# Smaller PE tiles in the first group, and weight loads on one queue, in a fused mLSTM and SwiGLU kernel

## The chip, the cores and the metric

The kernel runs on one core of a Trainium2 chip. Its time is device microseconds; three runs of the kernel before gave 514.97, 515.15 and 516.0, a median of 515.15. The engines are named as in the profile: PE (TensorE, matmuls), PEld (its weight loads), DVE (VectorE), ACT (ScalarE), POOL (GpSimd) and SP (SyncE, which here only issues transfers). ACT issues some transfers too. Each engine works through its own instructions in the order in which the program writes them.

## The reference

Two blocks follow each other. The first is an mLSTM cell over batch 4, 8 heads, 768 steps, head size 40; the second a SwiGLU feed-forward on its output, 3072 tokens of 320 features, hidden size 1536. All is float32.

```python
for t in range(S):
    kt, vt, qt = (k[:, :, t], v[:, :, t], q[:, :, t])
    m_new = np.maximum(f_gate[:, :, t] + m, i_gate[:, :, t])
    f_stab = np.exp(f_gate[:, :, t] + m - m_new)
    i_stab = np.exp(i_gate[:, :, t] - m_new)
    m = m_new
    C = f_stab[..., None, None] * C + i_stab[..., None, None] * np.einsum('bhd,bhe->bhde', vt, kt)
    n = f_stab[:, :, None] * n + i_stab[:, :, None] * kt
    h_tilde = np.einsum('bhde,bhe->bhd', C, qt)
    denom = np.maximum(np.abs(np.einsum('bhd,bhd->bh', n, qt)[:, :, None]), 1.0)
    y[:, :, t] = 1.0 / (1.0 + np.exp(-o_gate[:, :, t])) * h_tilde / denom
...
g = x @ w_gate
silu = g * (1.0 / (1.0 + np.exp(-g)))
return (silu * (x @ w_val)) @ w_out
```

The feed-forward weights reach the kernel as 64-bit floats in pairs of 32-bit words; the kernel makes float32 of them itself.

## The kernel before

**Groups.** The 768 steps are cut into six groups of 128 tokens (of each of the four sequences, so 512 tokens). For each group the kernel does the cell in chunk form (scores of k and q, decay weights, a product with v, and a state carried from chunk to chunk), turns the result x to features on partitions (xT), multiplies it with the gate and value weights, and the hidden values with the output weights. The cell of the next group is worked into the feed-forward of the one before. Groups 1 to 5 do their feed-forward products with seven half-size products in place of eight (`gated`, `project_seven`); group 0 does them plainly (`hidden` for each of 12 blocks m of 128 hidden features, then `project_all`).

**First group.** It has nothing to hide behind. Heads are handled in two halves P=0 and P=1 (sequences u=0, 1 and u=2, 3), 16 heads each. The steps named below are: `first_mask`, `first_inputs`, `first_maxima`, `first_exp` (the 128x128 decay weights W0, kept in h_sb[0:8]), `first_turn` (k and q to kT and qT, eight 128x128 transposes for each P and tensor, copied out of PSUM by two engines), `first_scores` (kT by qT, then DVE multiplies into W0), `first_own(u)` (W0 by v, 8 matmuls of 128x128 stationary and 41 moving columns in float32), `first_x(u)` (denominator and division on DVE), `first_gate(P)` (times the output gate), `first_seam(P)` (x to xT, ten 128x128 transposes), `first_state(P)` (k by weighted v, 128x64 tiles), `first_kept` (its copy to the state ring). `burn(n)` runs n bfloat16 matmuls whose result nobody reads. Later groups use forms of the same steps on 64-row tiles: `turn_one` and `seam`.

**PSUM.** Two rings of four banks: "cell" and "gen". `hidden(m)` takes two "gen" banks, so block m waits for the banks of block m-2, which are free when ACT (SiLU, line 688) and DVE (product, line 689) have read them. Scores and `add` share the "cell" ring.

**Weights.** They come in ten pieces (`PIECES`): pieces 0 and 1 are gate and value blocks 0 and 1, pieces 2 to 6 two blocks each (1280 KB), pieces 7 to 9 output weights. `piece_load` issues three transfers for a gate and value piece: the gate half to partitions 0 to 63 on SP, and the value half to partitions 64 to 127 in two transfers, on ACT for pieces 0 to 4 and on SP for the others. A piece lands in a raw buffer (a ring of two, `conv`) or in a "home" that is not used yet: h_sb[1:6] for piece 2, h_sb[8:13] for piece 3, wo_sb for piece 4. A block is then converted: `scale` on ACT (two instructions, lines 211 and 213), `join` on DVE (lines 220 and 221), `rounded` on POOL or DVE (line 228).

**Group 1 inside group 0's projections.** After each `hidden(0, m)` the list `slots[m]` is issued. Its order is the order on SP's queue as well. `late_sums` and `late_maxima` make M_sb, the running maxima of the later groups; these are written to a tensor in HBM (M_dram, line 933) and read back spread over partitions by `weights_load` (line 479) into w_sb. Slot 7 subtracts and masks w_sb (lines 483 and 488), slot 8 takes the exponential (line 492) and weighs the values, slot 9 does scores and multiplies them into w_sb (line 359), slot 10 runs `add` (line 378), slot 11 `attend`. `ahead[m]` names the blocks converted between the matmuls of m and its SiLU; block 8 is converted in m=5.

Of the kernel before, what the change touches and what calls it, by code (L numbers as in the profile page):

```python
# [12 lines left out]
U32 = mybir.dt.uint32  # L13
# [5 lines left out]
L = 128  # L19
# [5 lines left out]
def kernel(  # L25
# [50 lines left out]
    def bank(name, tag="cell"):  # L76
        return psum.tile([128, 512], F32, name=name, tag=tag)
# [77 lines left out]


    raws = {}
    PIECES = [("gv", 0, 1), ("gv", 1, 1)] + [("gv", m, 2) for m in range(2, NFC, 2)] + [("o", m, 4) for m in range(0, NFC, 4)]

    def piece_load(p, home=None):  # L160
        kind, m, n = PIECES[p]
        if kind == "gv":
            a, d = NKC, n * 128
            gate_w, val_w = (w[:, m * 128:(m + n) * 128].rearrange("(c p) f -> p c f", p=HP) for w in (moe_w_gate, moe_w_val))
            src = [(slice(0, HP), slice(0, NKC), gate_w), (slice(HP, 128), slice(0, NKC - 1), val_w[:, 1:]),
                   (slice(HP, 128), slice(NKC - 1, NKC), val_w[:, 0:1])]
            queues = (nc.sync,) + 2 * (nc.scalar if p < 5 else nc.sync,)
        else:
            a, d = n, DM
            src = [(slice(0, 128), slice(0, n), moe_w_out[m * 128:(m + n) * 128].rearrange("(a p) d -> p a d", p=128))]  # L170
            queues = (nc.sync,)
        if src[0][2].dtype == F32:
            for r, cs, w in src:
                if kind == "o":
                    nc.sync.dma_start(out=wo_sb[r, m:m + n, :], in_=w)
                else:
                    for x in range(n):
                        nc.sync.dma_start(out=wgv_sb[r, m + x, cs], in_=w[:, :, ts(x, 128)])
            return
        if home is None:  # L180
            raw = conv.tile([128, 4 * NKC * 128], U32, name="raw")
        else:
            raw = home.rearrange("p a t -> p (a t)").bitcast(U32)
        raw = raw[:, 0:2 * a * d]
        for (r, cs, w), queue in zip(src, queues):
            queue.dma_start(out=raw[r].rearrange("p (a d) -> p a d", a=a)[:, cs], in_=w.bitcast(U32))
# [122 lines left out]
    M_dram = tc.dram_tile([BH, S - L], F32, name="M_dram")  # L309


    def turn_one(P, src, dst, engs):
        tp = [bank("tp_kq").rearrange("p (a t) -> p a t", t=SUB) for _ in range(2)]
# [146 lines left out]
    def xT(n):  # L460
        return xT_sb
# [74 lines left out]
    def first_turn(P, src, dst, engs):  # L536
        for b in range(2):
            tp = bank("tp_kq").rearrange("p (a t) -> p a t", t=L)
            for a in range(UA // 2):
                h = P * UH + b * H + 2 * a  # L540
                nc.tensor.transpose(tp[:, a, :], src[:, h:h + 2, :].rearrange("p h d -> p (h d)"), ident)  # L541
            a = P * UA + b * UA // 2
            copy(engs[b], dst[:, a:a + UA // 2, :], tp)

    def first_scores(P):
# [13 lines left out]
    def first_own(u):  # L559
        first_y[u] = bank("first_y", "gen")[:, 0:H * D1].rearrange("p (h d) -> p h d", d=D1)  # L560
        for h in range(H):
            nc.tensor.matmul(first_y[u][:, h, :], lhsT=W0[:, u * H + h, :], rhs=v_sb[:, u * H + h, :], start=True, stop=True)  # L562

    def first_x(u):
        y = first_y.pop(u)
# [7 lines left out]
    def first_gate(P):  # L573
        for u in (2 * P, 2 * P + 1):
            x = x_sb[:, u, 0:DM].rearrange("p (h d) -> p h d", d=D)
            nc.vector.tensor_tensor(x, x, o_sb[:, u * H:(u + 1) * H], op=ALU.mult)
# [10 lines left out]
    def first_kept(P, ps, eng):  # L587
        copy(eng, state(2)[:, P * UA:(P + 1) * UA], ps)

    def first_seam(P, engs):  # L590
        for c, eng in zip(range(0, NKC, 2), engs):
            cs = range(c, min(c + 2, NKC))
            tp = bank("tp_x")[:, 0:len(cs) * 2 * L].rearrange("p (c u s) -> p c u s", u=2, s=L)
            for w in cs:
                for b in range(2):
                    nc.tensor.transpose(tp[:, w - c, b, :], x_sb[:, 2 * P + b, ds(w * HP, 2 * HP)], ident)
            copy(eng, xT(0)[:, c:c + len(cs), 2 * P * L:(2 * P + 2) * L].rearrange("p c (u s) -> p c u s", u=2), tp)
# [48 lines left out]
    piece_load(5)  # L646


    pair = early.tile([BH, PP], F32)
# [279 lines left out]
    def load_all(dst, a, n):  # L929
        for P in range(2):  # L930
# [7 lines left out]
    ahead[0] = []  # L938
    ahead.update({4: [6], 5: [7, 8], 6: [9], 7: [10], 8: [11], 9: [], 10: [], 11: []})
    slots = {  # L940
        0: [run(convert, 2, V), run(late_maxima), run(load_all, k_sb, k, 1),
            run(nc.sync.dma_start, out=M_dram, in_=flat(M_sb)), run(load_all, q_sb, q, 1)],
        1: [run(piece_load, 6), run(late_decay)],
        2: [run(nc.scalar.activation, step1, step1, AF.Exp), run(decay_rows), run(weights_load, 1), run(load_all, v_sb, v, 1)],
        3: [run(late_turns)],
        4: [run(decay)],
        5: [run(turn, 0, (A, A), (A, V))],
        6: [run(turn, 1, (A, A), (A, V)), run(piece_load, 7)],
        7: [run(weights_sub, 1, 0), run(weights_mask, 0), run(weights_sub, 1, 1), run(weights_mask, 1), run(nc.gpsimd.memset, q_sb, 0.0)],
        8: [run(weights_exp, 0), run(weights_exp, 1), run(weigh_values, G, 0), run(weigh_values, G, 1),  # L950
# [124 lines left out]
```

## Time and profile before

| | us |
|---|---|
| median of three runs (514.97 to 516.0) | 515.15 |
| the profiled execution | 516.62 |
| its span, first to last instruction | 514.8 |
| start of the first projection (line 683) | 31.62 |
| end of group 0's plain feed-forward, start of the first L831 | 126.2 |
| granted TensorE clock, share of full | 0.998 |

A line of a timeline gives the start, the length, the engine, the line of the program, the operation, what is written and read, the shapes and how many; in brackets, the idle time of the engine before it and who ended it. A group's length runs from its first start to its last end, so it can hold waits. SPq and ACTq are the queues that issue transfers: their length is the issue, not the transfer. The view of a line's instructions gives the time from issue to landing.

Waits of the first 95 us that bear on the parts that are changed:

```profile
ACT o_sb L495 <- DMA raw<-in_moe_w_val_dram: 4.7, 1, 4.7
...
DVE w_sb L483 <- DMA w_sb<-M_dram: 1.4, 1, 1.4
```

The columns are: who waited for whom, the sum in us, how often, the longest.

### The profile page before, as it was taken

The numbers are of one execution on the slowest core, as the hardware profiler recorded it, in microseconds if no ns is written. First come the engines' busy times: TensorE is split into PE (matmuls) and PEld (weight loads), VectorE is DVE, ScalarE is ACT, GpSimd is POOL, SyncE is SP. The second block draws the span as 40 slices with busy tenths as digits, with TensorE's granted clock in tenths as the row PEclk, the third lists the DMA queues.
The fourth block names the chain that finished last, engine by engine and source line by source line (L and its number), as shares of the span: only waits on it lengthen the run. The fifth ranks groups of instructions, "written<-read, shape, count | busy, mean of one in ns | idle before, by whom it ended". The sixth has DMA issues, their size and how long they took to land.

```text
span 514.8 us, 14725 instructions
## 1 busy us (share of the span) xinstructions
PE 506.3 (98%) x6309; PEld 430.3 (84%) x6309; DVE 345.3 (67%) x547; ACT 179.7 (35%) x269; POOL 279.2 (54%) x283
## 2 busy tenths in 40 slices
PE   8999999999999999999999999999999999999997
PEld 4964445667888889898899898999898899988896
DVE  5779666899858879857669656659666754233421
ACT  3377555434222244322335322345231330123210
POOL 1303327566399789457657457657347750166710
PEclk9999999999999999999999999999999999999999
DMA  9999999698100866700886600896700210100001
GB/s 126 176 241 221 171 215 216 148 180 94 52 3 12 153 101 76 105 3 6 132 127 76 107 3 3 122 138 77 108 4 1 34 21 20 33 1 1 0 14 39
DMA packets 205497, 43.28 MB, mean 84 GB/s; under 512 B 193432, under 2 KB 200600, under 8 KB 205432
## 3 DMA queue, kind: packets, MB, share of 16 engines
q1 hardware_dynamic: 203444, 39.49, 47.7%
q10 hardware_dynamic: 1988, 2.85, 2.4%
q8 instruction: 50, 0.82, 0.7%
q14 instruction: 15, 0.12, 0.1%
HBM read 35.68 MB, written 4.01 MB: 77 GB/s over the span
## 4 chain that ended last, share of the span: by engine, by line
PE 77%; DVE 11%; POOL 4%; issue 3%; DMA 2%; ACT 2%; SPq 1%; DVEq 0%; ACTq 0%; POOLq 0%
PE gv_x L831 23%; PE o_ps L754 20%; PE gv_y L831 18%; PE gv_ps L683 5%; DMA w_sb<-M_dram 2%; PE inter L401 2%; PE intra L406 2%; PE sp L352 2%; PE first_y L562 1%; POOL w_sb L488 1%; PE burn L501 1%; DVE vw_sb L419 1%; POOL tmp L872 1%; PE tp_kq L541 1%; PE sp L551 1%
## 5 line engine op out<-in xcount | busy, mean ns | idle before, releaser
L831 PE MATMUL gv_x<-xT,wgv_sb 64*128 64x256 f32 x720 | 93.7, 382 | 0.7 <-ACT tmp L881 0.4
L831 PEld LDWEIGHTS gv_x<-xT,wgv_sb 64*128 64x128 f32 x720 | 69.0, 187 | 9.0 <-issue 1.1
L754 PE MATMUL o_ps<-wo_sb,h_sb 128*128 128x160 f32 x480 | 67.4, 300 | 0.0
L754 PEld LDWEIGHTS o_ps<-wo_sb,h_sb 128*128 128x128 f32 x480 | 65.6, 190 | 1.7 <-issue 1.7
L683 PE MATMUL gv_ps<-xT,wgv_sb 64*128 64x512 f32 x240 | 53.5, 595 | 0.3 <-DVE wgv_sb L228 0.3
L488 POOL TENSOR_SCALAR_AFFINE_SELECT w_sb<-w_sb 64x1024 f32<-64x1024 f32 x20 | 31.1, 1555 | 25.3 <-DVE w_sb L483 16.8
L683 PEld LDWEIGHTS gv_ps<-xT,wgv_sb 64*128 64x128 f32 x240 | 23.5, 187 | 25.0 <-issue 23.5
L831 PE MATMUL gv_y<-q_sb,wgv_sb 64*128 64x256 f32 x360 | 44.1, 377 | 0.3 <-DVE x_sb L871 0.3
L831 PE MATMUL gv_y<-xT,wgv_sb 64*128 64x256 f32 x360 | 44.0, 376 | 0.0
L879 ACT ACTIVATE h_sb<-gv_x 128x256 f32<-128x256 f32 x30 | 11.5, 384 | 86.3 <-PE gv_x L831 86.2
L831 PEld LDWEIGHTS gv_y<-q_sb,wgv_sb 64*128 64x128 f32 x360 | 35.3, 187 | 4.2 <-DVE x_sb L871 0.7
L831 PEld LDWEIGHTS gv_y<-xT,wgv_sb 64*128 64x128 f32 x360 | 35.5, 187 | 3.4
L754 PE MATMUL o_ps<-wT,S 128*128 128x160 f32 x240 | 33.5, 300 | 0.1
L754 PEld LDWEIGHTS o_ps<-wT,S 128*128 128x128 f32 x240 | 32.8, 190 | 0.4 <-DVE tmp L768 0.4
L871 DVE TENSOR_TENSOR tmp<-tmp,gv_y 128x1024 f32<-128x1024 f32 x15 | 18.3, 1220 | 20.2 <-PE gv_y L831 18.3
L872 POOL TENSOR_TENSOR tmp<-tmp 128x512 f32<-128x512 f32 x15 | 20.0, 1335 | 21.1 <-DVE tmp L871 21.1
L831 PE MATMUL gv_x<-q_sb,sw 64*128 64x256 f32 x240 | 31.0, 376 | 0.0
L852 POOL TENSOR_TENSOR h_sb<-tmp 128x512 f32<-128x512 f32 x13 | 16.7, 1287 | 25.5 <-ACT tmp L851 25.5
L871 DVE TENSOR_TENSOR x_sb<-x_sb,gv_y 128x1024 f32<-128x1024 f32 x15 | 18.3, 1218 | 17.0 <-PE gv_y L831 16.1
L861 ACT COPY tmp<-gv_x 128x1024 f32<-128x1024 f32 x15 | 15.2, 1012 | 40.5 <-PE gv_x L831 40.5
L721 POOL TENSOR_TENSOR S<-h_sb 128x256 f32<-128x256 f32 x30 | 22.8, 759 | 9.2 <-DVE h_sb L852 7.3
L723 POOL TENSOR_TENSOR S<-S,h_sb 128x256 f32<-128x256 f32 x30 | 27.3, 911 | 0.0
(216 smaller groups left out, 1004.2 us busy)
## 6 DMA issues: line engine op xcount, KB each, us to landing
w_sb<-M_dram SPq DMA_DIRECT2D x10, 512.0 KB, 7.3
k_sb<-in_k_dram SPq DMA_DIRECT2D x12, 320.0 KB, 6.5
v_sb<-in_v_dram SPq DMA_DIRECT2D x12, 320.0 KB, 5.8
o_sb<-in_o_gate_dram SPq DMA_DIRECT2D x12, 320.0 KB, 6.3
raw<-in_moe_w_out_dram SPq DMA_DIRECT2D x3, 1280.0 KB, 7.6
x_sq<-k_sb SPq DMA_DIRECT2D x64, 40.0 KB, 2.0
q_sb<-in_q_dram SPq DMA_DIRECT2D x32, 64.0 KB, 2.5
out_dram<-tmp SPq DMA_DIRECT2D x24, 80.0 KB, 2.8
```

What stands on the lines that cost most here:

```text
L352: nc.tensor.matmul(sp[two][half(i), a, :], lhsT=kT[feats(two), P * UA + a, half(i)], rhs=qT[feats(two), P * UA + a, half(i)], start=True, ...
L488: nc.gpsimd.affine_select(w, w, compare_op=ALU.is_ge, fill=NEG, base=0, pattern=[[0, UH], [1, SUB]], channel_multiplier=-1)
L683: nc.tensor.matmul(ps[i], lhsT=wgv_sb[half(i), m, kc, :], rhs=x[half(i), kc, :], start=(kc == 0), stop=(kc == NKC - 1))
L721: eng.tensor_tensor(S1[:, k], lo[:, second_half], hi[:, second_half], op=ALU.add)
L723: eng.tensor_tensor(S2[:, k], S1[:, k], lo[:, first_half], op=ALU.subtract)
L754: nc.tensor.matmul(node[x][:, i], lhsT=lhs(k)[:, ts(i, L)], rhs=rhs(k), start=start and k == 0 and i == 0, stop=stop and k == KH - 1, skip ...
L831: nc.tensor.matmul(ps[:, i, cols], lhsT=lhs(c)[half(i)], rhs=rhs(c)[half(i)], start=start and c == 0, stop=stop and c == n - 1, skip_group ...
L852: (nc.vector if k == KH - 1 else nc.gpsimd).tensor_tensor(h_sb[:, 2 * k + 1], uw[:, 0], uw[:, 1], op=ALU.mult)
L861: nc.scalar.copy(uw, x)
L871: nc.vector.tensor_tensor(uw, uw, y, op=ALU.add)
L872: nc.gpsimd.tensor_tensor(uw[:, :, second_half], uw[:, :, second_half], uw[:, :, first_half], op=ALU.add)
L879: nc.scalar.activation(h[:, first_half], x[:, 0, first_half], AF.Silu)
```

## The change

Eight edits, in the diff below:

- `first_turn` is left for P=0 only; P=1 is turned by `turn_one`, sixteen 64-row transposes each for k and q.
- The 128x128 transposes of `first_seam` are gone; `seam` (twenty 64x64 tiles) does x for both P.
- `first_own` does each head in two halves of 64 columns, 16 matmuls for each u in place of 8.
- `first_gate` takes an engine: POOL for P=0, DVE for P=1.
- Burns are put in more places, 25 matmuls in all where there were 13; most go to the "gen" ring.
- All weight transfers are issued on SP's queue.
- Piece 1 shares piece 0's raw buffer, pieces 2 and 6 land in a free stretch of wo_sb (`spare_wo`), piece 4 in the raw ring.
- `late_sums` moves to the end of the first group, `late_maxima` from slot 0 to slot 1, `late_decay` from slot 1 to slot 2; piece 5 is issued in slot 0 behind the loads of k and q; M_dram is written in slot 1 behind piece 6, and its load stays in slot 2.

```diff
-            queues = (nc.sync,) + 2 * (nc.scalar if p < 5 else nc.sync,)
+            queues = (nc.sync,) + (nc.sync, nc.sync)
...
         if home is None:
-            raw = conv.tile([128, 4 * NKC * 128], U32, name="raw")
+            if p != 1:
+                raw = conv.tile([128, 4 * NKC * 128], U32, name="raw")
+                ring[p] = raw
+            else:
+                raw = ring[0][:, 2 * NKC * 128:]
...
+    spare_wo = wo_sb.rearrange("p m d -> p (m d)")[:, H * L:H * L + 4 * NKC * 128].rearrange("p (a t) -> p a t", a=1)
...
         for h in range(H):
-            nc.tensor.matmul(first_y[u][:, h, :], lhsT=W0[:, u * H + h, :], rhs=v_sb[:, u * H + h, :], start=True, stop=True)
+            for i in range(2):
+                nc.tensor.matmul(first_y[u][half(i), h, :], lhsT=W0[:, u * H + h, half(i)], rhs=v_sb[:, u * H + h, :],
+                                 start=True, stop=True)
...
-    first_turn(0, k_sb, kT, (V, V))
-    first_turn(0, q_sb, qT, (A, V))
+    first_turn(k_sb, kT, (V, V))
+    first_turn(q_sb, qT, (A, V))
     first_exp(1)
     first_values(0)
     first_scores(0)
-    first_own(0)
-    late_sums()
-    first_turn(1, k_sb, kT, (A, A))
-    first_x(0)
-    first_turn(1, q_sb, qT, (A, V))
+    burn(2, "gen")
+    turn_one(1, k_sb, kT, (A, A))
     load(o_sb, o_gate, 0, 1)
     piece_load(0)
+    burn(1, "gen")
+    first_own(0)
     first_own(1)
+    turn_one(1, q_sb, qT, (A, V))
     first_values(1)
+    first_x(0)
+    first_x(1)
+    burn(4, "gen")
     first_scores(1)
-    first_x(1)
     sig(0)
     piece_load(1)
-    burn(3)
+    piece_load(2, spare_wo)
+    burn(3, "gen")
     first_own(2)
-    piece_load(2, h_sb[:, 1:1 + NKC])
+    burn(1, "gen")
+    first_own(3)
+    first_gate(0, G)
     sig(1)
-    burn(2)
-    first_own(3)
-    first_gate(0)
+    seam(0, 0, (A, A, A, A))
     first_x(2)
     first_x(3)
-    first_gate(1)
-    first_seam(0, (A, A, V))
+    first_gate(1, V)
     scale(0)
-    ps1 = first_state(1, "gen")
-    burn(1, "gen")
+    states = [first_state(P, "gen") for P in range(2)]
+    burn(2, "gen")
     piece_load(3, h_sb[:, NH - NKC:])
     join(0)
-    first_seam(1, (A, A, V))
     rounded(0, V)
-    first_kept(0, first_state(0), A)
-    first_kept(1, ps1, V)
+    seam(0, 1, (A, V, A, V))
+    burn(5, "gen")
+    first_kept(0, states[0], A)
+    first_kept(1, states[1], V)
+    piece_load(4)
     convert(1, V)
+    late_sums()
     nc.scalar.activation(warm, warm, AF.Silu)
-    piece_load(4, wo_sb)
-    piece_load(5)
...
-        0: [run(convert, 2, V), run(late_maxima), run(load_all, k_sb, k, 1),
-            run(nc.sync.dma_start, out=M_dram, in_=flat(M_sb)), run(load_all, q_sb, q, 1)],
-        1: [run(piece_load, 6), run(late_decay)],
-        2: [run(nc.scalar.activation, step1, step1, AF.Exp), run(decay_rows), run(weights_load, 1), run(load_all, v_sb, v, 1)],
+        0: [run(convert, 2, V), run(load_all, k_sb, k, 1), run(load_all, q_sb, q, 1), run(piece_load, 5)],
+        1: [run(late_maxima), run(piece_load, 6, spare_wo), run(nc.sync.dma_start, out=M_dram, in_=flat(M_sb))],
+        2: [run(late_decay), run(nc.scalar.activation, step1, step1, AF.Exp), run(decay_rows), run(weights_load, 1), run(load_all, v_sb, v, 1)],
```

More of the change, by code (lines that the diff above doesn't have):

```diff
@@ L157 @@
     raws = {}
+    ring = {}
     PIECES = [("gv", 0, 1), ("gv", 1, 1)] + [("gv", m, 2) for m in range(2, NFC, 2)] + [("o", m, 4) for m in range(0, NFC, 4)]
@@ L309, with turn_one @@
     M_dram = tc.dram_tile([BH, S - L], F32, name="M_dram")
-    def turn_one(P, src, dst, engs):
-        tp = [bank("tp_kq").rearrange("p (a t) -> p a t", t=SUB) for _ in range(2)]
+    def turn_one(P, src, dst, engs, tag="cell"):
+        tp = [bank("tp_kq", tag).rearrange("p (a t) -> p a t", t=SUB) for _ in range(2)]
         for a in range(UA):
@@ L534, in first_values, with first_turn @@
                                 op=ALU.mult)
-    def first_turn(P, src, dst, engs):
+    def first_turn(src, dst, engs):
         for b in range(2):
@@ L539, in first_turn @@
             for a in range(UA // 2):
-                h = P * UH + b * H + 2 * a
+                h = b * H + 2 * a
                 nc.tensor.transpose(tp[:, a, :], src[:, h:h + 2, :].rearrange("p h d -> p (h d)"), ident)
-            a = P * UA + b * UA // 2
+            a = b * UA // 2
             copy(engs[b], dst[:, a:a + UA // 2, :], tp)
@@ L571, in first_x, with first_gate @@
                                 den.to_broadcast([128, H, D]), op=ALU.mult)
-    def first_gate(P):
+    def first_gate(P, eng):
         for u in (2 * P, 2 * P + 1):
             x = x_sb[:, u, 0:DM].rearrange("p (h d) -> p h d", d=D)
-            nc.vector.tensor_tensor(x, x, o_sb[:, u * H:(u + 1) * H], op=ALU.mult)
+            eng.tensor_tensor(x, x, o_sb[:, u * H:(u + 1) * H], op=ALU.mult)
         nc.gpsimd.tensor_copy(x_sb[:, 2 * P:2 * P + 2, DM:], x_sb[:, 2 * P:2 * P + 2, 0:HP])
@@ L588, in first_kept @@
         copy(eng, state(2)[:, P * UA:(P + 1) * UA], ps)
[L590 to L597, printed above, removed]
     burn(7)
@@ L940 @@
     slots = {
-        0: [run(convert, 2, V), run(late_maxima), run(load_all, k_sb, k, 1),
-            run(nc.sync.dma_start, out=M_dram, in_=flat(M_sb)), run(load_all, q_sb, q, 1)],
-        1: [run(piece_load, 6), run(late_decay)],
-        2: [run(nc.scalar.activation, step1, step1, AF.Exp), run(decay_rows), run(weights_load, 1), run(load_all, v_sb, v, 1)],
+        0: [run(convert, 2, V), run(load_all, k_sb, k, 1), run(load_all, q_sb, q, 1), run(piece_load, 5)],
+        1: [run(late_maxima), run(piece_load, 6, spare_wo), run(nc.sync.dma_start, out=M_dram, in_=flat(M_sb))],
+        2: [run(late_decay), run(nc.scalar.activation, step1, step1, AF.Exp), run(decay_rows), run(weights_load, 1), run(load_all, v_sb, v, 1)],
         3: [run(late_turns)],
+        5: [run(turn, 0, (A, A), (A, V))],
         4: [run(decay)],
-        5: [run(turn, 0, (A, A), (A, V))],
         6: [run(turn, 1, (A, A), (A, V)), run(piece_load, 7)],
```

## The prediction

> **What bounds the kernel now.** I read the busy times first. TensorE (PE) is busy 98% of the span and the transfers are busy in every slice up to about 90 us:
>
> ```profile
> PE 506.3 (98%) x6309; PEld 430.3 (84%) x6309; DVE 345.3 (67%) x547; ACT 179.7 (35%) x269; POOL 279.2 (54%) x283
> ...
> DMA  9999999698100866700886600896700210100001
> ```
>
> Everything after the first group is PE work without gaps worth naming, so whatever shift stands when PE has left the first projections stands at the end. Two places set that shift. The first is the end of the first group, in PE's timeline:
>
> ```profile
> 24.81 1.88 PE L562 MATMUL first_y<-v_sb,h_sb 128*128 128x41 f32 x16
> 26.52 1.29 PE L596 MATMUL tp_x<-ident,x_sb 128*128 128x128 f32 x10
> 27.73 1.13 PE L584 MATMUL add<-vw_sb,k_sb 128*64 128x41 f32 x32
> ...
> 31.62 17.61 PE L683 MATMUL gv_ps<-xT,wgv_sb 64*128 64x512 f32 x80 [0.28 <-DVE wgv_sb L228]
> ```
>
> The projections start when VectorE (DVE) has joined the first weight block. The second place is 50 us later, DVE's timeline and then PE's:
>
> ```profile
> 70.74 0.69 DVE L689 TENSOR_TENSOR h_sb<-tmp,gv_ps 128x512 f32<-128x512 f32 x1 [0.35 <-ACT tmp L688]
> 72.79 2.36 DVE L483 TENSOR_TENSOR w_sb<-g_T,w_sb 128x1024 f32<-128x1024 f32 x2 [1.36 <-DMA w_sb<-M_dram]
> ...
> 79.76 0.68 DVE L689 TENSOR_TENSOR h_sb<-tmp,gv_ps 128x512 f32<-128x512 f32 x1
> ...
> 84.49 2.48 DVE L359 TENSOR_TENSOR w_sb<-sp,w_sb 128x512 f32<-128x512 f32 x4
> ```
>
> ```profile
> 80.62 4.56 PE L683 MATMUL gv_ps<-xT,wgv_sb 64*128 64x512 f32 x20
> ...
> 85.82 2.33 PE L378 MATMUL add<-vw_sb,k_sb 64*64 64x41 f32 x126 [0.29 <-DVE w_sb L359]
> ```
>
> DVE stands 1.36 us for the load of w_sb from M_dram. Behind that wait, in DVE's order, is L689 of m=8, which ends at 80.44; it frees the PSUM banks that PE takes at 80.62 for m=10. So PE has 0.18 us in hand there, and at `add` (L378) it already waits 0.29 us for this chain. From the landing of w_sb (72.7) to `add` is 13.1 us of serial DVE, POOL, ACT and DVE work that the change leaves alone. **A later w_sb load is a later end, nearly one to one; an earlier PE gains nothing unless w_sb is earlier too.**
>
> What makes w_sb late is SP's queue, which is worked in order:
>
> ```profile
> 51.01 2.15 SPq L933 DMA_DIRECT2D M_dram<-M_sb  x1
> 53.20 2.63 SPq L137 DMA_DIRECT2D q_sb<-in_q_dram  x2
> 55.94 1.99 SPq L186 DMA_DIRECT2D raw<-in_moe_w_gate_dram  x1
> 57.97 1.28 SPq L186 DMA_DIRECT2D raw<-in_moe_w_val_dram  x2
> 59.35 7.34 SPq L479 DMA_DIRECT2D w_sb<-M_dram  x2
> ```
>
> Issue plus time to landing gives the service order: piece 4 lands at 45.6 (29.12 + 16.44), piece 5 at 51.7 (40.56 + 11.13), the last q at 60.9 (53.67 + 7.24), piece 6 at 67.15 (58.63 + 8.52), w_sb at 72.7 (59.97 + 12.72). Each starts where the one before lands, so this is a line without holes. The rates by stretch (busy time of PE, PEld, DVE, ACT, POOL; clock; DMA share; GB/s):
>
> ```profile
> 36.00:42.00 6.00, 6.00 (x31) 3.08 (x29) 4.83 (x8) 4.08 (x6) 0.00 (x0) 1.00 1.06 326
> 42.00:48.00 6.00, 6.00 (x30) 2.77 (x28) 5.86 (x12) 4.68 (x6) 2.59 (x2) 1.00 1.05 205
> 60.00:64.00 4.00, 4.00 (x32) 2.05 (x30) 3.03 (x6) 2.86 (x6) 1.55 (x1) 1.00 1.05 223
> ```
>
> In 36 to 42 us both queues move weights, SP's the gate halves to partitions 0 to 63, ACT's the value halves to 64 to 127 (60% and 46% of the engines' time by the queue view): 326 GB/s. In 42 to 48 SP's is alone: 205.
>
> **The change, part by part.**
>
> *PE work of the first group.* The turns of k and q for P=1: two of 8 transposes of 128x128 step 16.27 to 18.21, 1.94 us; the 64-row form (L317) steps two of 16 in 59.24 to 60.23, 0.99 us. Saved 0.95. The seam: 10 in 1.21 us (26.52 to 27.73) against 20 in 0.77 (L471, 109.16 to 109.93), twice: saved 0.88. `first_own` in two column halves has the shape of L584, 32 in 1.07 us (27.73 to 28.80), against 16 in 1.73 (24.81 to 26.52 and its like): saved 4 x 0.66 = 2.64. Burns go from 13 to 25; two took 0.44 (24.37 to 24.81), so +12 x 0.22 = 2.6 where no wait swallows them. PE alone: between -4.5 and -1.8 us.
>
> *DVE and ACT there.* DVE loses `late_sums` (1.47 us, now after the start of the projections) and the gating of P=0 (0.88, now on POOL, where 128x656 took 1.29, so two of 128x320 some 1.3). But DVE is busy from 23.7 to 31.5 almost without a hole: `first_x` of 2 and 3, the second gate, the join (0.49 + 0.82), the rounding (0.81). Laid out in the new order from the weighing of P=1 (about 23.7, as `first_x(1)` now precedes it) I get the rounding done at 30.2 and the last xT copies near 30.9. The projections start 0.6 to 1.0 us earlier; bounds 0 and 1.8 (PE's own saving), I take 0.8. It is eaten by w_sb below.
>
> *Value halves on SP's queue.* ACT no longer holds its own instructions behind a transfer (its sigmoid at 26.33 sat 4.66 us for that). The price is the overlap. Pieces 0 and 1 land no later (28.5 to 28.75 now, at 215 GB/s over 20 to 29 us with both queues, a rate that one queue has too). Pieces 2 to 4 are 3 x 1280 KB = 3.93 MB. One queue moved piece 5 (1.31 MB) in 6.13 us and piece 6 in 6.24, so 18.7 us from 28.75: piece 4 lands near 47.5 instead of 45.6, **+1.9 us**. Bounds: 0 if the overlap is worth nothing; 6 us x (326 - 205) GB/s = 0.73 MB, 3.5 us at 205, if all of it is lost.
>
> *Order in slots 0 to 2.* Piece 5 goes behind k and q, so it lands near 47.5 + 8.9 + 6.1 = 62.5 instead of 51.7. `scale(8)` reads it, at 57.38 on ACT, with the SiLU of m=5 and the copies of the first turn queued behind it; these then wait some 5 us, PE about 2 us at the second turn, for PSUM banks. That stall lies wholly before w_sb's and is not added.
>
> *M_dram behind piece 6.* Now it is written 8.3 us before its load is issued, with q and piece 6 covering the round trip. After the change the write stands directly ahead of the load, which must wait until it has landed, while nothing else is in the line: the v loads, pieces 7 and 8 and the second o load are queued behind it on SP. Piece 6 to w_sb took 67.15 to 72.70, 5.55 us, with the load waiting in the queue. The trace has one load issued to an emptied queue: 100.46, first half landed 5.4 us later; the second half follows the first by 1.8 to 2.5 us in the other groups, so 7.2 to 7.9. With 0.1 to 1 us for the write's own landing: 7.3 to 8.9 against 5.55. Bounds +1.7 and +3.4, I take +2.6; the write's 80 KB leaves the line ahead of piece 6, -0.3. What waits behind: v's user on POOL (L363) runs at 82.8 and itself waits for w_sb, so it costs nothing more; the later loads shift as PE does.
>
> *Other homes.* Pieces 1, 2, 4 and 6 get buffers free well before (piece 2's old home waited for `first_own(2)`). Nothing, under the line's cover; without it the 1.9 us that SP stood for it.
>
> **Sum.** w_sb lands 1.9 + 2.6 - 0.3 = 4.2 us later, near 77; PE stands at 63 and at m=10, and `add` comes 4.2 us later. 514.8 + 4.2 = 519.0 for the profiled span. That execution took 516.62 in all, 1.8 around the span, the median shown is 515.15; carried over: **519.4**.
>
> **Rivals.**
>
> 1. *The halves overlap for nothing.* The gain of 36 to 42 us comes back elsewhere (24 to 36 us had both queues at 200 to 237 GB/s), and only the round trip is paid: +2.3, 517.4. The 326 against 205 speaks against. The Trainium skill, SBUF — State Buffer, "Can I just issue two DMAs to hit both halves?", says that one transfer at partition 0 and one at 64 together gave only 6% over one; by that rule this rival would be the case, and the trace's 59% disagrees.
> 2. *The round trip is hidden,* if the write overtakes piece 6 in the engines' rings. Only the overlap is paid: +1.6 to 1.9, 517.
> 3. *PE goes cold.* It stands 2 to 3 us twice. The seven first burns took 3.17 us, 0.45 each against 0.22 later: another such stretch costs some 1.6 us: 521.0. No wait over 1.2 us shows here, so the rows can't settle it.
> 4. *Faster.* The line ahead of w_sb shortens: ACT's transfers no longer share the engines with SP's, and SP no longer stands at 22 to 24.6 us. If w_sb lands before 71.9 despite the new order, PE's 0.8 us (to 1.8) persists: 513.4 to 514.4, say 514.3. Below that landing time it decides. Against it: the bytes ahead are the same and the line has no holes.
>
> **Chances.** Forecast 0.62, first rival 0.12, second 0.05, third 0.08, fourth 0.09, nothing within reach of measuring 0.04. About 0.2%, 1 us, is what this kernel's measurement tells from none. Faster 0.09, same 0.06, slower 0.85. The range leaves the lower edge of the fourth and the upper of the third out: 514.1 to 522.5. The forecast's own, from its bounds, is 516.5 to 521.5.
>
> **What would show it.** Right: the load of w_sb issued at 70 or later, DVE's idle before L483 grown from 1.36 to over 4 us, no stretch at 300 GB/s before 48 us, PE idle before the m=10 block. L683 starts at 30.6 to 31.0. Wrong: L483 starting before 73, or PE without idle time between 60 and 90 us.

## The result and the profile after

| | before | after |
|---|---|---|
| median of five runs each, us | 515.15 (514.87 to 518.13) | 521.23 (520.88 to 521.32) |
| the profiled execution | 516.62 | 520.88 |
| its span | 514.8 | 519.1 |
| first projection (L683, now L685) starts | 31.62 | 31.90 |
| piece 4 / piece 6 / w_sb landed | 45.6 / 67.15 / 72.70 | 49.11 / 70.22 / 77.68 |
| `add` (L378, now L384), its long group starts | 85.82 | 90.81 |
| first L831 (now L833) starts | 126.17 | 130.53 |

The ratio is 1.0103, with a 95% interval of 1.0075 to 1.0131: slower by some 5 us. Landings are the issue plus the time to landing, as in the prediction. The line numbers have moved: L483 is now L489, L359 is L365, L689 is L691, L211 is L216, L317 is L323.

The page of the changed kernel, busy times, clock and DMA by slices of 13 us, and the two queues (packets, MB, share of the transfer engines' time):

```profile
PE 508.9 (98%) x6421; PEld 429.0 (83%) x6421; DVE 344.1 (66%) x545; ACT 179.3 (35%) x271; POOL 281.1 (54%) x285
...
PEclk9999989999999999999999999999999999999999
DMA  9999999798300696700686800696800110100001
...
q1 hardware_dynamic: 205204, 42.11, 50.0%
q10 hardware_dynamic: 228, 0.23, 0.2%
```

PE is again busy 98% of the span, so its share says nothing. What has changed is one digit of the clock, in the slice from 65 to 78 us, and the second queue (q10, ACT's), which moves next to nothing now. PE's timeline:

```profile
31.90 17.44 PE L685 MATMUL gv_ps<-xT,wgv_sb 64*128 64x512 f32 x80 [0.64 <-DVE xT L143]
...
66.91 0.27 PE L323 MATMUL tp_kq<-ident,k_sb 64*128 64x64 f32 x1 [1.92 <-ACT kT L141]
67.39 0.71 PE L323 MATMUL tp_kq<-ident,k_sb 64*128 64x64 f32 x15 [0.21 <-ACT kT L141]
67.89 0.72 PE L323 MATMUL tp_kq<-ident,q_sb 64*128 64x64 f32 x16
68.43 14.79 PE L685 MATMUL gv_ps<-xT,wgv_sb 64*128 64x512 f32 x60
...
85.18 4.85 PE L685 MATMUL gv_ps<-xT,wgv_sb 64*128 64x512 f32 x20
90.22 0.31 PE L384 MATMUL add<-vw_sb,k_sb 64*64 64x41 f32 x2 [0.18 <-DVE w_sb L365]
90.81 2.33 PE L384 MATMUL add<-vw_sb,k_sb 64*64 64x41 f32 x126 [0.29 <-DVE w_sb L365]
```

PE stands 1.92 us at the second turn, and the 60 matmuls behind it take 14.79 us where another execution of the kernel before took 13.09. It still arrives at `add` before the chain of w_sb does. That chain, on SP's queue and then on DVE:

```profile
58.57 0.53 SPq L935 DMA_DIRECT2D M_dram<-M_sb  x1
70.43 2.03 SPq L485 DMA_DIRECT2D w_sb<-M_dram  x2
72.55 4.59 SPq L137 DMA_DIRECT2D v_sb<-in_v_dram  x2
```

```profile
65.25 0.49 DVE L225 TENSOR_SCALAR wgv_sb<-top 128x640 uint32<-128x640 uint32 x1 [6.95 <-ACT top L216]
...
77.78 2.36 DVE L489 TENSOR_TENSOR w_sb<-g_T,w_sb 128x1024 f32<-128x1024 f32 x2 [1.78 <-DMA w_sb<-M_dram]
```

The write of M_dram lands at 70.41 and the load is issued 0.02 us later. From the landing of w_sb to `add` it is 13.13 us (90.81 - 77.68), as it was before (85.82 - 72.70 = 13.12). By stretches (columns as in the prediction):

```profile
36.00:42.00 6.00, 6.00 (x31) 3.05 (x30) 4.70 (x7) 3.94 (x6) 2.32 (x3) 1.00 1.06 213
...
69.00:72.00 3.00, 3.00 (x10) 1.14 (x8) 2.83 (x5) 3.00 (x7) 0.00 (x0) 0.52 0.09 25
```

The 326 GB/s of 36 to 42 us have become 213. In 69 to 72 us the transfers all but stop (25 GB/s), while SP waits for the write (to 70.41) and the load behind it gets under way; in the same stretch PE's clock is 0.52.

So w_sb came 4.98 us later: 3.07 because piece 6 landed later, and 1.91 because w_sb now takes 7.46 us from there instead of 5.55. `add` followed with 4.99. By the first L833, 4.36 is left: a wait of 1.15 us in the traced execution before, at L406, for which the profile shows no reason, is not there in this one, which loses some 0.4 us at L477 instead. The span grew by 4.3.

### The profile page after: what moved, and what is told of

Read it like the earlier page. It is cut to its first block, busy times and chain, and to the rows that moved or that the text cites. A ratio compares the mean times of both kernels' runs of the same rounds, so it can differ in the third digit from the quotient of the medians.

```text
span 519.1 us, 14948 instructions
## 1 busy us (share of the span) xinstructions
PE 508.9 (98%) x6421; PEld 429.0 (83%) x6421; DVE 344.1 (66%) x545; ACT 179.3 (35%) x271; POOL 281.1 (54%) x285
## 4 chain that ended last, share of the span: by engine, by line
PE 75%; DVE 4%; DMA 4%; POOL 2%; issue 2%; ACT 2%; SPq 0%; DVEq 0%; ACTq 0%; POOLq 0%
PE gv_x L833 24%; PE o_ps L756 21%; PE gv_y L833 19%; PE o_ps L702 5%; DMA M_dram<-M_sb 2%; PE inter L407 2%; PE intra L412 2%; PE sp L358 2%; POOL w_sb L494 1%; DMA w_sb<-M_dram 1%; PE gv_ps L685 1%; DMA q_sb<-in_q_dram 1%; ACT L690 0%; DVE w_sb L365 0%; POOL tmp L874 0%
## 5 line engine op out<-in xcount | busy, mean ns | idle before, releaser
L833 PE MATMUL gv_x<-xT,wgv_sb 64*128 64x256 f32 x720 | 93.6, 382 | 0.9 <-ACT tmp L883 0.4
L833 PEld LDWEIGHTS gv_x<-xT,wgv_sb 64*128 64x128 f32 x720 | 69.0, 187 | 9.2 <-issue 1.1
L685 PE MATMUL gv_ps<-xT,wgv_sb 64*128 64x512 f32 x240 | 55.3, 609 | 0.6 <-DVE xT L143 0.6
L685 PEld LDWEIGHTS gv_ps<-xT,wgv_sb 64*128 64x128 f32 x240 | 25.7, 192 | 25.4 <-issue 22.6
L833 PE MATMUL gv_y<-q_sb,wgv_sb 64*128 64x256 f32 x360 | 44.1, 377 | 0.3 <-DVE x_sb L873 0.3
L833 PE MATMUL gv_y<-xT,wgv_sb 64*128 64x256 f32 x360 | 44.0, 376 | 0.0
L833 PEld LDWEIGHTS gv_y<-q_sb,wgv_sb 64*128 64x128 f32 x360 | 35.2, 187 | 4.2 <-DVE x_sb L873 0.7
L833 PEld LDWEIGHTS gv_y<-xT,wgv_sb 64*128 64x128 f32 x360 | 35.4, 187 | 3.5
L833 PE MATMUL gv_x<-q_sb,sw 64*128 64x256 f32 x240 | 31.0, 376 | 0.0
```

Of the source, the lines that this page charges most:

```text
L685: nc.tensor.matmul(ps[i], lhsT=wgv_sb[half(i), m, kc, :], rhs=x[half(i), kc, :], start=(kc == 0), stop=(kc == NKC - 1))
L833: nc.tensor.matmul(ps[:, i, cols], lhsT=lhs(c)[half(i)], rhs=rhs(c)[half(i)], start=start and c == 0, stop=stop and c == n - 1, skip_group ...
```

## The experiments

Each run was compared with the kernel before on the same chip; the kernel before gave medians of 516.78, 515.69 and 516.32 us on three chips, with single runs from 514.4 to 519.1. The first four rows ran on the first chip, the next four on the second, the last four on the third. "Piece 6" and "w_sb" are their landings (a blank where the trace has no record of it), and "`add`" is the start of its long group (of the whole, where PE came to it without a wait).

| run | median, us | ratio (95% interval) | span | piece 6 | w_sb | `add` |
|---|---|---|---|---|---|---|
| e1 order back | 519.05 | 1.0048 (1.0031 to 1.0066) | 516.9 | 70.58 | 75.03 | 88.89 |
| e2 queue back | 524.16 | 1.015 (1.0127 to 1.0173) | 522.6 | 68.82 | 77.82 | 94.93 |
| e3 both back | 526.33 | 1.0185 (1.0162 to 1.0208) | 524.7 | 69.54 | 74.34 | 96.85 |
| e4 kernel before | 515.81 | 0.9988 (0.9971 to 1.0005) | 512.9 | 66.25 | 70.30 | 85.52 |
| e5 before, one queue | 518.78 | 1.0053 (1.0035 to 1.007) | 516.5 | 71.41 | 75.60 | 88.73 |
| e6 before, M_dram late | 518.13 | 1.0035 (1.0015 to 1.0056) | 513.7 | 65.47 | 72.87 | 86.01 |
| e8 before, ACT has all value halves | 526.66 | 1.0213 (1.0191 to 1.0235) | 524.5 | 69.14 | 73.93 | 96.75 |
| e9 two queues, later pieces | 520.05 | 1.0077 (1.006 to 1.0094) | 518.2 | 66.97 | 72.20 | 90.61 |
| e10 M_dram early | 519.81 | 1.0085 (1.0059 to 1.0111) | 517.8 | 71.20 | 75.41 | 89.54 |
| e11 e10 and POOL's queue | 518.12 | 1.0041 (1.002 to 1.0062) | 514.8 | | 73.75 | 87.12 |
| e12 e10, w_sb ahead of piece 6 | 522.30 | 1.0123 (1.0101 to 1.0145) | 520.9 | 76.02 | 69.38 | 92.45 |
| e13 before, `first_own` in halves | 518.11 | 1.0046 (1.0023 to 1.007) | 515.7 | 68.42 | 73.83 | 86.95 |

### The kernel before once more (e4)

The file has one empty line more.

> The kernel before once more, for a second trace: the traced execution took 516.6 where the median is 515.15. Theory: a typical execution has w_sb landing about 1.5 us earlier than the traced one (71.2 for 72.7), since with two queues the overlap of the halves differs from run to run; ratio 1.000. Rival: its transfers are the same and PE's first matmuls run at half rate for longer in one than in the other, so that wps starts or ends over 1 us apart.

The time is the same, but this execution (514.71, second fastest of twelve) differs from the one that the prediction was made from. PE's timeline, then DVE's:

```profile
65.98 13.09 PE L683 MATMUL gv_ps<-xT,wgv_sb 64*128 64x512 f32 x60
79.00 2.09 PE L352 MATMUL sp<-qT,kT 40*64 40x64 f32 x128
81.03 4.56 PE L683 MATMUL gv_ps<-xT,wgv_sb 64*128 64x512 f32 x20
85.52 2.08 PE L378 MATMUL add<-vw_sb,k_sb 64*64 64x41 f32 x128
```

```profile
71.15 0.69 DVE L689 TENSOR_TENSOR h_sb<-tmp,gv_ps 128x512 f32<-128x512 f32 x1 [0.89 <-ACT tmp L688]
71.76 2.35 DVE L483 TENSOR_TENSOR w_sb<-g_T,w_sb 128x1024 f32<-128x1024 f32 x2
```

w_sb landed at 70.30, DVE came to it 1.5 us later without a wait, and `add` ran as one group of 128: PE sets the end here, and w_sb has 85.52 - 70.30 - 13.1 = 2.1 us in hand. In the profiled execution of the table above w_sb landed at 72.70 and set the end by a little. The kernel before stands at the border of the two.

### One queue alone (e5), and the order alone, undone (e1) and done (e6)

e5 is the kernel before with all value halves on SP's queue and nothing else:

```diff
-            queues = (nc.sync,) + 2 * (nc.scalar if p < 5 else nc.sync,)
+            queues = (nc.sync,) + (nc.sync, nc.sync)
```

> The kernel before with one line changed: all value halves on SP's queue. Theory (the overlap of the halves is what is lost): no stretch above 300 GB/s before 60 us, piece 6 lands at 69 to 71 where the two traces of the kernel before have 67.15 and 66.25, w_sb at 74 to 75; the last q lands near 64 as in the run with the order put back, so PE waits about 2 us for it; 517.5 to 519.5. Rival (halves overlap for nothing): piece 6 by 67.2, 515 to 516.5.

PE's timeline, then DVE's:

```profile
62.07 0.71 PE L317 MATMUL tp_kq<-ident,q_sb 64*128 64x64 f32 x16 [1.61 <-DMA q_sb<-in_q_dram]
...
88.73 2.33 PE L378 MATMUL add<-vw_sb,k_sb 64*64 64x41 f32 x126 [0.29 <-DVE w_sb L359]
```

```profile
75.69 2.36 DVE L483 TENSOR_TENSOR w_sb<-g_T,w_sb 128x1024 f32<-128x1024 f32 x2 [0.45 <-DMA w_sb<-M_dram]
```

Piece 4 lands at 48.80 (45.6 and 43.8 in the two traces before), piece 6 at 71.41 (67.15 and 66.25), w_sb at 75.60; DVE waits for it and PE for DVE, 13.13 us later. One queue alone costs 3.1 us against the median of that chip, and no stretch reaches 300 GB/s (36 to 42 us show 210). The Trainium skill, SBUF — State Buffer, "Can I just issue two DMAs to hit both halves?", has two transfers at partitions 0 and 64 only 6% above one. This run disagrees: taking the second queue away made piece 4 later by 3.2 to 5.0 us. The trace of before agrees with it in part: its two queues moved 326 GB/s in 36 to 42 us, but 200 to 237 in 24 to 36, which is one queue's rate.

e6 is the kernel before with the write of M_dram moved behind piece 6, and nothing else:

```diff
-            run(nc.sync.dma_start, out=M_dram, in_=flat(M_sb)), run(load_all, q_sb, q, 1)],
-        1: [run(piece_load, 6), run(late_decay)],
+            run(load_all, q_sb, q, 1)],
+        1: [run(piece_load, 6), run(nc.sync.dma_start, out=M_dram, in_=flat(M_sb)), run(late_decay)],
```

> The kernel before with M_dram written behind piece 6, nothing else. Theory (the round trip is paid in full): piece 6 lands as before, 66 to 67, from there to w_sb 7.5 us and not 4.1 to 5.6; w_sb at 73.7 to 74.6, the add block 13.1 us later at 86.8 to 87.7 where it was 85.5 and 85.8, the time 516.5 to 517.5. Rival (the write overtakes piece 6): w_sb by 72.7, 515 to 516.

```profile
72.97 2.36 DVE L483 TENSOR_TENSOR w_sb<-g_T,w_sb 128x1024 f32<-128x1024 f32 x2 [1.34 <-DMA w_sb<-M_dram]
```

That is DVE's timeline. Piece 6 landed at 65.47, the write at 65.64, the load was issued at 65.65 and landed at 72.87: 7.40 us from piece 6, where the two traces before have 4.05 and 5.55. So the round trip adds 1.9 to 3.4 us to w_sb; with the 2 us in hand little of that reached this execution (515.51, the fastest of twelve from 515.51 to 520.66), while the median rose by 2.4. Expected were w_sb at 73.7 to 74.6 and a time of 516.5 to 517.5: the landing came earlier than that, with piece 6, and the median is 0.6 above it.

e1 is the changed kernel with slots 0 to 2, and piece 5 ahead of k and q, as before; the queue stays.

```diff
-        0: [run(convert, 2, V), run(load_all, k_sb, k, 1), run(load_all, q_sb, q, 1), run(piece_load, 5)],
-        1: [run(late_maxima), run(piece_load, 6, spare_wo), run(nc.sync.dma_start, out=M_dram, in_=flat(M_sb))],
+        0: [run(convert, 2, V), run(late_maxima), run(load_all, k_sb, k, 1),
+            run(nc.sync.dma_start, out=M_dram, in_=flat(M_sb)), run(load_all, q_sb, q, 1)],
+        1: [run(piece_load, 6, spare_wo), run(late_decay)],
...
     nc.scalar.activation(warm, warm, AF.Silu)
+    piece_load(5)
```

> The changed kernel with the order of slots 0 to 2 and the place of piece 5 as before; the value halves stay on SP's queue. Theory (the landing of w_sb sets the end; its 5.0 us of delay are 3.1 us of lost overlap, piece 6 landing at 70.2 and not 67.15, and 1.9 us of round trip): piece 6 to w_sb falls from 7.5 to about 5.5 us, w_sb lands near 75.8, the time falls by 1.9 to about 519.3, and ACT's 7.5 us stand for piece 5 is gone. Rival (the first group's own new steps cost the time, the order costs nothing because other transfers move meanwhile): 521 unchanged.

```profile
61.77 0.71 PE L323 MATMUL tp_kq<-ident,q_sb 64*128 64x64 f32 x16 [1.90 <-DMA q_sb<-in_q_dram]
...
88.89 2.08 PE L384 MATMUL add<-vw_sb,k_sb 64*64 64x41 f32 x128
```

In PE's timeline the loss of the overlap shows in another place: q, now behind piece 5, lands after PE has come to need it (its second half at 64.37), and PE waits. Behind that wait of 1.90 us the granted clock is 0.50 from 63.0 to 66.4 us. Piece 6 to w_sb is back at 4.45 us, and `add` runs without a wait, 0.8 us after w_sb would have allowed it (75.03 + 13.1): here PE is the bound. Undoing the order takes the ratio from 1.0103 to 1.0048, about half of the loss.

e1 and e5 differ by the new first group alone, with its homes for the pieces. Their ratios, 1.0048 and 1.0053, are the same within their intervals, so the new first group neither costs nor gains a time that these runs can tell. One queue alone costs 0.53% (e5) and the late write alone 0.35% (e6), together 0.88 of the change's 1.03%; piece 5 behind k and q has no run of its own.

### The queue undone with ACT (e2, e3, e8, e9): a wait of another kind

e2 is the changed kernel with the value halves of pieces 0 to 4 on ACT's queue again (the first line of the diff, reversed); e3 is e1 and e2 together; e8 is the kernel before with all value halves on ACT (`2 * (nc.scalar,)`).

> The changed kernel with the value halves of pieces 0 to 4 on ACT's queue again; order and first group as changed. Theory: a stretch above 300 GB/s comes back before 45 us, piece 6 lands near 67, w_sb near 74.6, the time falls by 3.1 to about 518.1. Rival (two halves together move no faster than one after the other): no such stretch, piece 6 still near 70, 521.

> The changed kernel with both undone, so the new first group alone (smaller PE tiles, burns, homes). Theory: w_sb lands within 0.5 us of before, so the time is that of before within 1 us, 514.3 to 516: PE's own 0.9 us at the start of the projections is lost in the wait for w_sb. Rival (the new first group itself is slower): 517 or more. Rival (PE's start sets the end): 514.2 or less with w_sb landing no earlier.

> The kernel before with the value halves of all gate and value pieces on ACT's queue, 5 and 6 too. Theory (two halves at once move at over 300 GB/s, and w_sb has slack then): piece 6 lands before 64, w_sb before 69, DVE doesn't wait for it, PE alone sets the end: 513.5 to 515.2, with less spread. Rival (ACT's compute is held behind its own issues, as in the two runs that put the value halves back on ACT in the new order): ACT idle ahead of a SiLU over 2 us, PE waits, 517 or more.

All three became slower than the changed kernel, and my expectations fell; in e8 the rival came out, ACT held behind its own issues. e3's rival of a slower first group has the time, but not the cause: e1 and e5 speak against it, and the same sigmoid waits 8.34 us in e3. ACT's timeline in e2:

```profile
27.86 4.71 ACTq L191 DMA_DIRECT2D wo_sb<-in_moe_w_val_dram  x2
32.61 0.74 ACT L501 ACTIVATE o_sb<-o_sb 128x640 f32<-128x640 f32 x1 [8.33 <-DMA wo_sb<-in_moe_w_gate_dram]
```

ACT's sigmoid stands 8.33 us behind two issues of ACT itself, which wait for a landing of SP's. The operands of the transfers in the trace say why. SP's and ACT's transfers take eight semaphores in turn, as the program gives them, to report that they have landed, one set for both, and an issue waits until the transfer that had its semaphore last has landed. Piece 2's second value transfer here takes semaphore 109 and is issued at 32.08; the last with 109 was piece 2's gate half, which landed at 32.05. In the new first group more transfers are issued ahead of that sigmoid, so it waits longer than the 4.66 us of before, and the projections start at 38.45 (e2) and 40.50 (e3). In e8 it is the SiLU, later (ACT's timeline, then PE's):

```profile
46.57 0.60 ACT L688 ACTIVATE tmp<-gv_ps 128x512 f32<-128x512 f32 x1 [11.13 <-DMA wo_sb<-in_moe_w_gate_dram]
```

```profile
50.24 10.55 PE L683 MATMUL gv_ps<-xT,wgv_sb 64*128 64x512 f32 x40 [8.31 <-DVE wgv_sb L228]
```

So these runs say nothing against the overlap (with both queues at work, 30 to 36 us show 283 GB/s in e2 and 309 in e3, where no 2 us of the changed kernel from 30 to 48 show over 220); they show a second price of ACT's queue, which the change does take away.

e9 tried to have both: the new first group with pieces 0 to 2 on SP's queue, the value halves of pieces 3 to 6 on ACT's, issued from the end of the first group on, M_dram early and piece 5 ahead of k.

```diff
+            queues = (nc.sync,) + 2 * (nc.scalar if p > 2 else nc.sync,)
...
-    piece_load(3, h_sb[:, NH - NKC:])
     join(0)
...
-    piece_load(4)
...
     nc.scalar.activation(warm, warm, AF.Silu)
+    piece_load(3, h_sb[:, NH - NKC:])
+    piece_load(4)
...
+        0: [run(convert, 2, V), run(piece_load, 5), run(late_maxima), run(load_all, k_sb, k, 1),
```

> The new first group with pieces 0 to 2 wholly on SP, the value halves of 3 to 6 on ACT, issued from the end of the first group on where ACT has room; M_dram written early, piece 5 ahead of k. Theory (nothing is wrong with the new first group, it only lacked transfers in time): the projections start at 30.7 to 31.5, w_sb lands before 69, PE has no wait over 0.5 us up to 100 us, 512.5 to 514.5, faster than both. Rival (ACT is held by its issues): a SiLU waits over 2 us, 516 or more. Rival (the first group saves nothing): 515 with w_sb in time.

The answer on who waited for whom (sum, times, longest):

```profile
ACT tmp L690 <- DMA h_sb<-in_moe_w_gate_dram: 6.6, 1, 6.6
...
PE gv_ps L685 <- DVE wgv_sb L233: 3.5, 1, 3.5
```

w_sb landed at 72.20, 5.5 us earlier than in the changed kernel, but ACT was held again, PE stood, and `add` came at 90.61 bound by PE. The forecast of 512.5 to 514.5 fell, and the rival came out.

### M_dram early, and a queue that holds nobody (e10, e11)

e10 is the changed kernel with `late_maxima` and the write of M_dram back in slot 0, ahead of q; k and q stay ahead of piece 5. e11 adds POOL's queue for two pieces.

```diff
-        0: [run(convert, 2, V), run(load_all, k_sb, k, 1), run(load_all, q_sb, q, 1), run(piece_load, 5)],
-        1: [run(late_maxima), run(piece_load, 6, spare_wo), run(nc.sync.dma_start, out=M_dram, in_=flat(M_sb))],
+        0: [run(convert, 2, V), run(late_maxima), run(load_all, k_sb, k, 1),
+            run(nc.sync.dma_start, out=M_dram, in_=flat(M_sb)), run(load_all, q_sb, q, 1), run(piece_load, 5)],
+        1: [run(piece_load, 6, spare_wo)],
...
+            queues = (nc.sync,) + 2 * (nc.gpsimd if p in (3, 4) else nc.sync,)
```

> The changed kernel with the write of M_dram back ahead of q in slot 0 (and late_maxima with it); queue, homes, first group and the order k, q, piece 5 stay. Theory (landing of w_sb sets the end; the round trip costs what the two order experiments showed): piece 6 still lands at 70 to 71, w_sb 4 to 5.5 us later, 74.5 to 76 in place of 77.7, so add near 88 and the time 2 to 3 us under the changed kernel's: 518 to 519. PE has no wait for q, unlike with piece 5 ahead of q. Rival (with PE late behind piece 5 for its own reasons, through scale(8)): w_sb is early but add stays at 90.8 and the time at 520.5 to 521.5.

> The kernel of the run before, with the value halves of pieces 3 and 4 on POOL's queue, which is a second queue that holds no ACT. POOL has no work between 28.4 and 41.8 us but 2.2 us at 36. Theory (two queues that fill the two partition halves move 300 GB/s and more where one moves 205; what spoilt the runs with ACT's queue was ACT's own work behind the issue): 36 to 48 us show more than 280 GB/s, piece 4 lands near 45 in place of 49, piece 6 near 66.5, w_sb near 71, add is bound by PE at 85 to 86, and the time is 514.5 to 516. Rival 1 (two queues give nothing, the 326 GB/s had another source): landings as in the run before, 518 to 519. Rival 2 (POOL is held like ACT): rounding of piece 2 on POOL, at 41.8 in the changed kernel, comes 3 us or more later, PE waits for it, 519 to 523.

e10, ACT's timeline and then PE's:

```profile
64.45 0.77 ACT L216 ACTIVATE top<-raw 128x640 f32<-128x640 f32 x1 [7.99 <-DMA raw<-in_moe_w_val_dram]
```

```profile
66.92 0.27 PE L323 MATMUL tp_kq<-ident,k_sb 64*128 64x64 f32 x1 [2.25 <-ACT kT L141]
...
89.54 2.08 PE L384 MATMUL add<-vw_sb,k_sb 64*64 64x41 f32 x128
```

w_sb lands at 75.41, as expected, 2.3 us earlier than in the changed kernel, but `add` only 1.3: it is PE now that comes at 89.54, late by the stall behind piece 5. The time (519.81) lies between what the theory and its rival gave. So behind the chain of w_sb a second bound stands, 1.3 us lower, and undoing the first alone gives no more than that.

e11, POOL's timeline and then two stretches:

```profile
28.20 1.32 POOL L191 DMA_DIRECT2D h_sb<-in_moe_w_val_dram  x2
29.52 1.16 POOL L191 DMA_DIRECT2D raw<-in_moe_w_val_dram  x2
35.98 0.62 POOL L302 MEMSET keep<- 32x640 f32 x1 [5.31 <-DVE f_sb L301]
```

```profile
36.00:42.00 6.00, 4.75 (x24) 2.06 (x21) 2.92 (x6) 3.03 (x5) 2.12 (x2) 1.00 1.03 281
42.00:48.00 6.00, 5.86 (x26) 2.50 (x28) 5.51 (x8) 3.90 (x6) 1.58 (x2) 1.00 1.05 151
```

POOL issues its four transfers in 2.5 us and is not held: they have semaphores of their own and none waits for another. 36 to 42 us show 281 GB/s, as the theory said; 42 to 48, for which it said the same, show 151, and piece 4 lands at 47.34, where it had 45. The first half of k lands at 48.70 in place of 51.35. But piece 2, which now shares with the halves of piece 3, lands at 38.67 in place of 36.14, and PE waits 1.25 us for its block; and SP issues the write of M_dram, with q behind it, at 46.80, only 1.1 us earlier than in e10, so that 1.6 us reach piece 5 (62.71 for 64.35). No wait of PE and no cold stretch are left at the second turn, w_sb lands at 73.75 and `add` is at 87.12, 2.4 us before e10's. The median is 1.7 below e10's; it misses the forecast of 514.5 to 516, and the kernel before is still faster (ratio 1.0041). The traced execution, 516.52, is the third fastest of twelve (515.96 to 520.89), so a typical one has less than the 2.4 us.

### The load of w_sb ahead of piece 6 (e12)

```diff
+        1: [run(weights_load, 1), run(piece_load, 6, spare_wo)],
...
+    ahead.update({4: [6], 5: [7, 8], 6: [9], 7: [], 8: [10], 9: [11], 10: [], 11: []})
```

> The kernel of e10 with the load of w_sb issued ahead of piece 6, and blocks 10 and 11 converted one block later, since piece 6 lands later. One queue for all weights stays. Theory: piece 5 lands near 64.5, w_sb near 69 to 70, piece 6 near 75.5; then w_sb no longer sets the end, add is bound by PE at 85 to 87, and the time is 515 to 517, although the overlap of the queues is still lost. Rival (piece 6 sets it then, or ACT's stall for piece 5 does): PE waits 2 us or more for block 10 or before m=8, add near 88 to 89, 518 to 519.

PE's timeline:

```profile
68.08 1.60 PE L323 MATMUL tp_kq<-ident,k_sb 64*128 64x64 f32 x16 [2.64 <-ACT kT L141]
...
91.86 0.31 PE L384 MATMUL add<-vw_sb,k_sb 64*64 64x41 f32 x2 [1.40 <-DVE w_sb L365]
```

w_sb lands at 69.38 and piece 6 at 76.02, as expected, but the time rose: PE stands for piece 5 all the same, goes cold (clock 0.61 in 69 to 72 us), and the later conversion of blocks 10 and 11 now lies on DVE ahead of L365. With one queue the line of transfers is too long for any order that was tried: what goes ahead makes the next in it late.

### Less PE work in the first group alone (e13)

The kernel before with `first_own` in two halves of 64 columns, as in the change, and nothing else.

> The kernel before with first_own alone in 128x64 halves (64 matmuls in place of 32 x 2 at half length). The first group's PE work in that row falls from 7.5 to some 4 us in all. Theory (DVE is the bound of the first group, PE waits for it): the projections start 0 to 0.6 us earlier, w_sb lands where it did, the time is that of the kernel before within 0.5 us (515.2 to 516). Rival (PE is the bound there): the projections start 1.5 to 2.6 us earlier and the time falls to 513 to 514.

PE's timeline, then ACT's:

```profile
24.80 1.43 PE L598 MATMUL tp_x<-ident,x_sb 128*128 128x128 f32 x10
...
29.42 1.51 PE L598 MATMUL tp_x<-ident,x_sb 128*128 128x128 f32 x10 [1.81 <-DVE x_sb L578]
...
33.01 17.49 PE L685 MATMUL gv_ps<-xT,wgv_sb 64*128 64x512 f32 x80 [1.01 <-DVE wgv_sb L228]
```

```profile
28.02 0.74 ACT L495 ACTIVATE o_sb<-o_sb 128x640 f32<-128x640 f32 x1 [5.86 <-PE burn L501]
```

PE reaches the first seam 1.7 us earlier than before (26.52), and the projections start 1.4 us later. The releaser that the profile names for the sigmoid had long been done; ACT's own issue for piece 2 sat until 27.48, for the gate half of piece 0 that landed at 27.39 (25.69 in the trace of before). Piece 2's home, h_sb, is free earlier with the faster `first_own`, so its gate half was issued at 23.34 instead of 24.62. That it took the engines from piece 0 is what these times suggest; no run separates it from the spread of executions. What is shown is that PE's saving alone does not make the projections start earlier, and both expectations fell. The three other traces of the kernel before or of its first group (e4, e5, e6) start the projections at 31.95 to 32.33, so part of the 1.4 us is spread.

## Why the prediction was right, point by point

- **What sets the end.** The landing of w_sb plus 13.1 us: right in the changed kernel to 0.01 us, and in e5 and e6 as well. What the prediction took from one trace, that the kernel before is bound there too, holds for that execution and not for every one: in e4 PE sets the end and w_sb has 2.1 us in hand.
- **Value halves on one queue: the term that was too small.** "+1.9 us" came from 18.7 us for pieces 2 to 4, counted from 28.75. Piece 4 landed 3.55 us later (49.11 for 45.56), the upper bound, and piece 6, with 0.3 taken off for the write, was to be 1.6 later and was 3.07. The rate was right: piece 2 landed at 36.66, and pieces 3 and 4 took 6.16 and 6.29 us from there. The start was not: "Pieces 0 and 1 land no later" holds for piece 1's gate half (28.73) alone. Its value halves now stand behind it in the same line, and piece 2 landed 7.9 us after 28.73 instead of 6.2. The value halves have no landing on record, so how the 1.7 us divide stays open. e5 confirms the term by itself.
- **The round trip.** Forecast 7.3 to 8.9 us from piece 6 to w_sb, measured 7.46 and, in e6, 7.40: right at the lower end, +1.9 against the trace of before where +2.6 was taken. Undone, it is 4.2 to 4.5 us (e1, e10).
- **The sum.** +4.2 at w_sb was forecast, +4.98 measured; 0.6 of this was met by the unexplained 1.15 us of the execution before, so that the span's 519.1 stands beside 519.0. That agreement is closer than the terms are.
- **The median.** Forecast 519.4, measured 521.23. Of the 6.08 us, 4.26 separate the two profiled executions, 1.47 is that the profiled execution before was slower than its median, and 0.35 that the one after was faster than its own. The execution before was one in which w_sb is late, and it was taken for the typical one; e4 shows another, 1.9 us faster. The five runs of the changed kernel lie within 0.44 us, as they would if every execution waited for w_sb; one trace shows that wait. To carry the shift of a slow trace over to the median was the step that left the forecast 1.8 short.
- **Piece 5 behind k and q.** "These then wait some 5 us, PE about 2 us": 7.46 on ACT, 1.92 and 0.21 on PE. Not adding it was right, and e10 shows how narrowly: without the round trip this stall is the bound, 1.3 us lower.
- **First group.** The projections were to start at 30.6 to 31.0 and started at 31.90. The warm-up of that execution took 1.17 us longer (L518, 3.32 us for 2.15), so up to 0.9 us of gain may be in it. Counted from the end of the warm-up, the projections start after 24.4 to 25.0 us in the changed kernel, e1 and e9 to e12, and after 25.2 to 25.7 in the two traces of the kernel before, e5 and e6: a gain of 0.8 in the mean, which is what was taken. No run shows it as a gain in time.
- **The signs.** DVE's idle before L489 was not over 4 us but 1.78: the stall behind piece 5 had pushed DVE's own work up to the landing, and the rest of its idle time is the 6.95 before L225. PE did not stand before the block of m=10; the cold clock had stretched what was ahead of it.
- **The rivals.** Overlap for nothing: falls by e5. Round trip hidden: falls by the load issued at 70.43, 0.02 us after the write's landing. PE cold: it happened (0.52 of the clock, 14.79 us for 13.09, so 1.7, priced at 1.6), but under the wait for w_sb, where it costs nothing; in e1, e10 and e12, where PE stood 1.90, 2.25 and 2.64 us, it came again, and in e1 and e10 it is part of the bound. Faster: w_sb landed 5.8 us above the point from which it would have decided.

What stays open: why two queues moved 326 GB/s in 36 to 42 us and no more than one in 24 to 36, and whether it is the two queues or the two partition halves that count, since no run had two queues fill the same half; why executions of one kernel differ by up to 4.7 us on one chip, in the landings above all, and what the waits of 0.3 to 1.2 us at L401, L406 and L412 are that some executions show.

## What to carry to other kernels

Follow the transfer that is waited for last back through its queue, with the landing of each transfer ahead of it, and cost an edit by what it puts into that line; a write and the load that reads it back belong as far apart in the line as their data allow. When the bound is undone, look at once for the next: here it lay 1.3 us lower, so neither half of the change, undone alone, gave the time back. Before a shift is taken from one trace, take a second one of the same kernel: where two bounds stand within the spread of executions, one trace shows only one of them.

## What the runs showed of the hardware

In these kernels an issue on ACT's or SP's queue waits for the landing of an earlier transfer on either, through the eight semaphores that they share in turn, and what the engine computes waits behind it: 8.33 us (e2) and 11.13 us (e8) of ACT. POOL's four issues took 2.5 us and held nothing (e11).

Some 2 us without work were enough for the lower clock. In the changed kernel 3.44 us lie between two projections, 1.92 and 0.21 of them idle and 1.3 with 64-row transposes only; then the granted clock is 0.50 from 68.5 to 71.9 us. In e1 2.91 us between two projections, 1.90 of them idle, did the same from 63.0 to 66.4. In e5, with 2.62 us between them and 1.61 idle, the clock stayed full. The Trainium skill, TensorE: Matmul & The Clock Gate, "What's actually happening", names an idle window of about 3.4 us. The length of the cold stretches agrees, 3.41 us in the changed kernel and in e1; that so long an idle time is needed does not, for in both 1.9 us were enough, and in e1 the 3.4 us ahead of the lower clock hold 0.7 us of projections.
